# Attention and a gated feed-forward on one core: masks added ahead of the scores, and the casts and loads of the first units reordered

## The chip, the core and the metric

The kernel runs on one core of a Trainium2 chip. A core has five engines with an instruction queue each, which run beside each other and wait for each other through semaphores: TensorE (PE, with its weight loads listed as PEld), VectorE (DVE), ScalarE (ACT), GpSimd (POOL) and SyncE (SP). Transfers between memory and the core go through DMA queues; SyncE, ScalarE and GpSimd issue them. The metric is the device time of one execution in microseconds; lower is better.

## The reference

The inputs are q, k and v (4 batches, 8 heads, 768 positions, 64 values), the list of retrieval heads (0, 2 and 6), and the weights of a feed-forward (512 to 2048 to 512).

```python
scores = scale * np.matmul(q, k.transpose(0, 1, 3, 2))
stream_keep = causal & (is_sink | in_win)        # 4 sink positions, a window of 64
mask = np.where(retr[...], causal, stream_keep)  # by head
a = softmax(np.where(mask, scores, -1e9))
x = (a @ v).transpose(0, 2, 1, 3).reshape(3072, 512)
h = x @ w_in
out = (h * sigmoid(beta * h)) @ w_out
```

## The kernel before, in words

**Units and chunks.** A chunk is one half (384 positions) of one batch; chunks 0 and 1 are the first halves of batches 0 and 1, chunk 2 is the second half of batch 0. Each chunk has four units; unit p handles the two heads p and p+4. So units 0 to 7 are the first two chunks, and there are 32 in all. A retrieval head needs all causal blocks of 128 by 128; a streaming head needs a few, some against a copy of K and V (KO, VO) whose first four rows are the sink.

**What a unit does.** `load_qk` (L123) brings q and k of two units into a staging tile `s`; `load_v` (L143) brings V. `cast` (L286) makes bf16 of them (tile `qkb`). `steps_T` (L361) transposes on TensorE into two PSUM banks (three 128-column transposes for K, three for Q), and copies them out: KT on VectorE (L371), and the two heads' halves of QTP, first on ScalarE, then on VectorE (L378). `sinks_of` (L342) makes KO, on GpSimd for most units. `steps_QK` (L440) cuts the unit's 10 or 11 blocks into three fills; a fill takes one PSUM bank, TensorE computes the scores into it (L464), and ScalarE takes the exponential (L472). `values` (L302) casts V into VX (L300) and makes VO (L313, L314). `steps_PV` (L478) multiplies (L495) and VectorE divides by the sums (L498, L500). `steps_X` (L517) transposes the result into xT.

**Masks.** For units 0 to 7 a masked block gets a second matmul behind its scores, with the identity as weights, which adds a tile of zeros and -1e9 (L469): Nc for a causal diagonal, parts of Ns for streaming heads. Ns and Mc are made by `negatives` (L217). Later units multiply the exponentials by 0 and 1 on VectorE (L437, with Mc and Mh).

**The feed-forward.** `steps_G1` (L550) gives groups of four matmuls x @ w_in (L560), a tanh on ScalarE (L563) and a gate on VectorE (L566). `steps_G2` (L573) gives the second product (L604). `ms(n)` puts n such groups between attention steps. w_in and w_out are cast while they are loaded, by transfers that GpSimd issues (L162, L166).

**Order.** Everything is issued in an order written out by hand for the first units (L706 to L827). Each engine does its instructions in that order, and a queue that waits holds back all that stands behind. PSUM has eight banks; `Banks` hands them out in turn: scores from 0 and 1, idle matmuls, G1 and some fills from 2 to 4, transposes from 5 and 6, PV from 7. A tile in a bank waits until the readers of the tile before it are done. Ten matmuls of zeros (`idle`, L186) stand ahead of everything on TensorE. A load into a staging buffer that was used before waits for a one-column memset by GpSimd (`held=True`).

Of the kernel before, what the change touches and what calls it, by code (L numbers as in the profile page):

```python
# [17 lines left out]
def kernel(  # L18
# [69 lines left out]
    def later(delay, fn):  # L88

        todo = [fn]  # L90

        def once():
            if todo:
                todo.pop()()
        heapq.heappush(heap, (clock[0] + delay, count[0], once))
        count[0] += 1
        return once
# [5 lines left out]
    def step(s):  # L103
        cost, fn = s
        flush(clock[0])
        clock[0] += cost
        fn()
# [15 lines left out]
    def load_qk(c, g, pairs=1, held=False):  # L123

        b, h2 = chunks[c]
        rows = slice(h2 * HALF, (h2 + 1) * HALF)
        both = stage.tile([128, 2, 2, 2, HT, D], F32, name=f"s{g}")
        for i, (name, src) in enumerate((("k", k), ("q", q))):
            staged[name, c, g] = both[:, i]
            if held:  # L130
                nc.gpsimd.memset(staged[name, c, g][:, 0, 0, 0, 0:1], 0.0)
        n = 2 // pairs
        for i in range(pairs):
            for name, src in (("k", k), ("q", q)):
                h = 2 * g + n * i
                eng = nc.scalar if pairs == 2 and name == "q" else nc.sync
                for hs in [slice(0, 2)] if n == 1 else [slice(0, 1), slice(1, 2)]:
                    eng.dma_start(
                        out=staged[name, c, g][:, n * i:n * (i + 1), hs].rearrange("p a h t d -> p (a h) (t d)"),
                        in_=src[b].rearrange("(c a) s d -> a c s d", c=2)[h:h + n, hs, rows, :].rearrange(  # L140
                            "a c (p t) d -> p a c (t d)", t=HT)[:, 0 if n == 1 else slice(0, n), slice(0, 2) if n == 1 else 0])
# [16 lines left out]
    def load_w_in(i, n=1):  # L158
        f = slice(i * 512, (i + n) * 512)
        view = moe_w_in.rearrange("(c a d) f -> c d a f", c=2, a=MO)  # L160
        for c in range(2):
            nc.gpsimd.dma_start(out=w_in_sb[c * D:(c + 1) * D, :, f], in_=view[c][:, :, f])  # L162
# [4 lines left out]
        w_done.add(i)  # L167

    load_qk(0, 0, 2)
    load_qk(0, 1)  # L170
    warm = consts.tile([1, 1], F32, name="warm")
    nc.vector.memset(warm, 0.0)
    nc.scalar.activation(out=warm, in_=warm, func=ACTF.Exp)
# [12 lines left out]
    def idle(n, pool, name):  # L186
        for i in range(n):
            nothing = pool.tile([128, 512], F32, name=name)
            nc.tensor.matmul(nothing, zeros[:, 0:128], zeros, start=True, stop=True)  # L189
    idle(10, ps_m, "mm")  # L190

    def select(buf, cm, step_, base, n):
        nc.gpsimd.affine_select(out=buf, in_=buf, compare_op=ALU.is_ge, fill=0.0, base=base,
# [21 lines left out]
    nc.gpsimd.affine_select(out=Nc, in_=Nc, compare_op=ALU.is_ge, fill=NEG, base=0, pattern=[[1, 128]], channel_multiplier=-1)  # L215

    def negatives():  # L217
        nc.vector.tensor_scalar(out=Mc, in0=Nc, scalar1=0.0, scalar2=None, op0=ALU.is_ge)
        for i, m in enumerate([M0, Mo, Md, Mo, Md]):
            nc.vector.tensor_scalar(out=Ns[:, i * 128:(i + 1) * 128], in0=m, scalar1=-1.0, scalar2=-NEG, op0=ALU.add, op1=ALU.mult)  # L220

# [7 lines left out]

    QTD = [kvp.tile([128, NPAIR, HALF], BF16, name=f"QTD{i}") for i in range(2)]  # L230
    QTP = kvp.tile([128, 3, 2, HALF], BF16, name="QTP")
    QTB = [[QTP[:, i, hh, :] for hh in range(2)] for i in range(3)]

    KT, KO, VX, VO = {}, {}, {}, {}
# [26 lines left out]
    def ones_v(eng, b):  # L261
        for p in range(NPAIR):
            eng.memset(VX[b, p][:, :, :, D:D + 1], 1.0)
            if streams[p]:
                eng.memset(VO[b, p][:, :, :, D:D + 1], 1.0)

    for i in range(3):
        zero_q(i)
    ones_v(nc.vector, 0)
    ones_v(nc.gpsimd, 1)  # L270

    def masks_late(h2):

        m = Mh[h2].rearrange("p (r k j) -> p r k j", r=2, j=128)
        res = []
        if h2 == 0:
            res.append(lambda: nc.vector.tensor_copy(out=m[:, :, 0], in_=M0[:, None, :].to_broadcast([128, 2, 128])))
        n = HT - 1 + h2
        for i, one in ((1 - h2, Mo), (2 - h2, Md)):
            for r in range(2):  # L280
                res.append(lambda i=i, one=one, r=r: nc.vector.tensor_copy(
                    out=m[:, r, i:i + 2 * n - 1:2], in_=one[:, None, :].to_broadcast([128, n, 128])))
        return res
# [12 lines left out]
    def cast_v(u):  # L296
        b, h2, p = units[u]
        c = u // NPAIR
        copy = nc.vector.tensor_copy if u in (0, 1, 2, 3, 5, 7) or 8 <= u < 16 else nc.gpsimd.tensor_copy
        copy(out=VX[b % 2, p][:, h2 * HT:(h2 + 1) * HT, :, 0:D], in_=staged["v", c][:, :, p:H:NPAIR, :])  # L300

    def values(u):  # L302
# [115 lines left out]
    def masks_of(es, lst, h2):  # L418

        res = []  # L420
        i = 0
        while i < len(lst):
            j = i + 1
            if lst[i][5]:
                while j < len(lst) and lst[j][5]:
                    j += 1
                res.append((i, j, Mc[:, None, :].to_broadcast([128, j - i, 128])))
            elif lst[i][6] is not None:
                while j < len(lst) and lst[j][6] == lst[j - 1][6] + 1:
                    j += 1  # L430
                m = lst[i][6]
                res.append((i, j, Mh[h2][:, m * 128:(m + j - i) * 128].rearrange("p (n j) -> p n j", j=128)))
            i = j

        def one(i, j, m):
            e = es[:, i * 128:j * 128].rearrange("p (n j) -> p n j", j=128)
            nc.vector.tensor_mul(e, e, m)  # L437
        return [lambda x=x: one(*x) for x in res]

    def steps_QK(u):  # L440

        b, h2, p = units[u]
        s = st_u.setdefault(u, {})
        s["masks"] = []
        s["blocks"] = blocks = [[[] for _ in range(HT)] for _ in range(2)]
        lst = sum(blocks_of(u), [])
        nb = len(lst)
        nf = -(-nb // 4)
        cuts = [nb * i // nf for i in range(nf + 1)]

        def fill(lo, hi, spare):
            def go():
                s["sinks"]()

                sp = (ps_s3 if u >= 10 else ps_m if spare else ps_s).tile([128, 512], F32, name="sp")
                es = att.tile([128, 512], BF16, name="es", bufs=NES)
                for i in range(lo, hi):
                    blocks[lst[i][0]][lst[i][3]].append((es[:, (i - lo) * 128:(i - lo + 1) * 128], lst[i][4]))
                i = lo
                while i < hi:  # L460
                    j = run_end(lst, i, hi)
                    hh, _, lhs, q0, _, diag, m = lst[i]
                    added = u < 8 and (diag or m is not None)
                    nc.tensor.matmul(sp[:, (i - lo) * 128:(j - lo) * 128], lhs, s["QT"][hh][:, q0 * 128:(q0 + j - i) * 128],  # L464
                                     start=True, stop=not added)
                    if added:

                        neg = Nc if m is None else Ns[:, m % 5 * 128:(m % 5 + 1) * 128]
                        nc.tensor.matmul(sp[:, (i - lo) * 128:(i - lo + 1) * 128], ident, neg, start=False, stop=True)  # L469
                    i = j  # L470
                w = (hi - lo) * 128
                nc.scalar.activation(out=es[:, 0:w], in_=sp[:, 0:w], func=ACTF.Exp, scale=scale)  # L472
                if u >= 8:
                    s["masks"] += [later(700, f) for f in masks_of(es, lst[lo:hi], h2)]
            return ((hi - lo) * (56 if u >= 8 else 95), go)
        return [fill(cuts[i], cuts[i + 1], (u < 4 or u in (6, 7)) and i % 2) for i in range(nf)]

    def steps_PV(u):  # L478
        b, h2, p = units[u]
# [208 lines left out]
    def transposes_of(u):  # L688
        step(steps_T(u)[0])
# [11 lines left out]
    def cast_dp(u):  # L701
        cast(u, "k", dve)
        cast(u, "q")
# [2 lines left out]
    act = nc.scalar.copy  # L706
    cast_dp(0)
    load_v(0, held=True)
    load_qk(1, 0)
    negatives()  # L710
    transposes_of(0)
    st_u[0]["sinks"]()
    cast(1, "k", act)
    cast(1, "q")
    qk = steps_QK(0)
    step(qk[0])
    transposes_of(1)
    step(qk[1])
    step(qk[2])
    st_u[1]["sinks"]()  # L720
    cast_dp(2)
    cast_dp(3)
    qk = steps_QK(1)
    step(qk[0])
    transposes_of(2)
# [8 lines left out]
    step(qk[1])  # L734
    step(qk[2])
    st_u[2]["sinks"]()
    load_qk(1, 1, held=True)
    st_u[3]["sinks"]()
    run(steps_QK(3))
    load_v(1, held=True)  # L740
# [11 lines left out]
    run(steps_PV(3))  # L752
    step(steps_X(1)[0])
    transposes_of(4)
    step(steps_X(2)[0])
    qk = steps_QK(4)
    step(qk[0])
    step(steps_X(3)[0])
    step(qk[1])
    transposes_of(5)  # L760
    nc.vector.memset(w_in_sb[:, 0, 512:513], 0.0)
    step(qk[2])
    qk = steps_QK(5)
    step(qk[0])
    load_w_in(1)
    cast(6)
    cast(7)
    load_w_in(2, 2)
    ms(1)
# [303 lines left out]
```

## Time and profile before

| what | us |
|---|---|
| median of 3 runs | 232.85 (232.28 to 233.64) |
| the profiled execution | 232.27 |
| its span, which the profile shows | 230.6 |
| around the span | 1.67 |
| TensorE busy | 219.8 (95%) |
| ScalarE, VectorE, GpSimd busy | 155.8, 145.1, 100.1 |
| first idle matmul on TensorE | 1.29 |
| first transposes, unit 0 | 5.54 |
| start of the steady run of L560 | 34.98 |

All places in time are microseconds from the start of the span. A line of the timeline has the start, the time until the last of its instructions ends, the engine, the source line, the operation, out<-in, shapes and a count; a bracket gives the idle time of the engine just before it and who ended it. In the windows view a row is a stretch of time: its length, each engine's busy time with its number of instructions, the granted clock, the DMA share and the bytes moved.

### The profile page before, as it was taken

The numbers are of one execution on the slowest core, as the hardware profiler recorded it, in microseconds if no ns is written. First come the engines' busy times: TensorE is split into PE (matmuls) and PEld (weight loads), VectorE is DVE, ScalarE is ACT, GpSimd is POOL, SyncE is SP. The second block draws the span as 40 slices with busy tenths as digits, with TensorE's granted clock in tenths as the row PEclk, the third lists the DMA queues.
The fourth block names the chain that finished last, engine by engine and source line by source line (L and its number), as shares of the span: only waits on it lengthen the run. The fifth ranks groups of instructions, "written<-read, shape, count | busy, mean of one in ns | idle before, by whom it ended". The sixth has DMA issues, their size and how long they took to land.

```text
span 230.6 us, 5311 instructions
## 1 busy us (share of the span) xinstructions
PE 219.8 (95%) x1940; PEld 132.2 (57%) x1960; DVE 145.1 (63%) x367; ACT 155.8 (68%) x304; POOL 100.1 (43%) x218
## 2 busy tenths in 40 slices
PE   7788899999999999999999999999999999999994
PEld 2676675654666666545654565454755556556553
DVE  6795787984768589745954593454781676338700
ACT  2788888882757898567875757684938797128621
POOL 6373780067698999057618692850052000000000
PEclk9999999999999999999999999999999999999999
DMA  6999999999999999968999899962832101211012
GB/s 195 257 183 271 152 155 192 227 209 234 222 185 137 176 135 186 154 133 98 161 194 139 139 182 151 143 126 70 184 53 63 50 0 45 81 47 50 0 45 91
DMA packets 95771, 31.78 MB, mean 138 GB/s; under 512 B 82673, under 2 KB 92289, under 8 KB 95745
## 3 DMA queue, kind: packets, MB, share of 16 engines
q0 software_dynamic: 35424, 8.13, 50.8%
q1 hardware_dynamic: 59456, 22.72, 46.6%
q10 hardware_dynamic: 864, 0.60, 0.8%
q8 instruction: 15, 0.25, 0.5%
q14 instruction: 12, 0.09, 0.2%
HBM read 27.27 MB, written 6.29 MB: 146 GB/s over the span
## 4 chain that ended last, share of the span: by engine, by line
PE 81%; DMA 5%; DVE 5%; ACT 4%; POOL 3%; issue 2%; SPq 1%; ACTq 0%; POOLq 0%
PE tp L604 32%; PE mm L560 31%; PE po L495 5%; PE sp L935 4%; DMA vs<-in_v_dram 3%; PE sp L464 2%; PE mm L189 2%; DMA xT<-x 2%; PE tp L587 2%; PE tp L369 1%; ACT es L939 1%; DVE QTP L378 1%; POOL w_in_sb L162 1%; ACT QTP L378 1%; DVE gT L566 1%
## 5 line engine op out<-in xcount | busy, mean ns | idle before, releaser
L560 PE MATMUL mm<-xT,w_in_sb 128*128 128x384 bf16 x512 | 92.3, 326 | 0.4 <-DMA xT<-x 0.2
L604 PE MATMUL tp<-w_out_sb,gT 128*128 128x512 bf16 x348 | 86.7, 379 | 1.3 <-issue 0.3
L563 ACT ACTIVATE th<-mm,beta_h 128x384 f32<-128x384 f32 x128 | 73.1, 598 | 20.3 <-PE mm L560 14.7
L566 DVE SCALAR_TENSOR_TENSOR gT<-th,mm 128x384 bf16<-128x384 f32 x128 | 67.4, 550 | 30.0 <-ACT th L563 25.7
L560 PEld LDWEIGHTS <-w_in_sb 128*128 128x128 bf16 x512 | 47.9, 98 | 31.7 <-issue 0.6
L604 PEld LDWEIGHTS <-gT 128*128 128x128 bf16 x368 | 33.9, 98 | 33.9 <-issue 0.4
L939 ACT ACTIVATE es<-sp 128x512 bf16<-128x512 f32 (+1 forms) x84 | 39.9, 594 | 4.5 <-PE sp L935 4.5
L611 ACT ACTIVATE osb<-tp 128x512 f32<-128x512 f32 x21 | 12.7, 603 | 31.5 <-PE tp L604 28.4
L472 ACT ACTIVATE es<-sp 128x512 bf16<-128x512 f32 (+1 forms) x44 | 22.9, 560 | 6.1 <-PE sp L464 4.8
L495 PEld LDWEIGHTS <-es 128*128 128x128 bf16 x472 | 20.6, 97 | 8.1 <-issue 0.7
L300 POOL CAST VX<-vs 128x384 bf16<-128x384 f32 x18 | 9.2, 521 | 35.7 <-DMA vs<-in_v_dram 23.4
L326 POOL DMA_DIRECT2D s<-in_q_dram x30 | 22.5, 768 | 0.4 <-issue 0.3
L326 POOL DMA_DIRECT2D s<-in_k_dram x30 | 22.3, 770 | 0.1
L495 PE MATMUL po<-VX,es 128*128 128x65 bf16 x392 | 22.2, 193 | 0.0
L437 DVE TENSOR_TENSOR es<-es,Mh 128x512 bf16<-128x512 bf16 (+3 forms) x58 | 19.4, 368 | 4.4 <-ACT es L939 3.7
L500 DVE TENSOR_TENSOR x<-po,rec 128x384 bf16<-128x384 f32 x32 | 17.8, 558 | 1.1
L464 PE MATMUL sp<-QTP,KT 128*128 128x128 bf16 (+2 forms) x113 | 16.6, 230 | 1.2 <-ACT QTP L378 1.1
L437 DVE TENSOR_TENSOR es<-es,Mc 128x384 bf16<-128x384 bf16 (+2 forms) x21 | 7.3, 351 | 11.3 <-ACT es L939 10.8
L294 POOL CAST qkb<-s 128x384 bf16<-128x384 f32 x14 | 6.8, 510 | 16.7 <-DMA s<-in_q_dram 14.4
L352 POOL COPY KO<-KT 128x128 bf16<-128x128 bf16 (+1 forms) x20 | 8.8, 440 | 9.8 <-DVE KT L371 4.4
L498 DVE RECIPROCAL rec<-po 128x6 f32<-128x6 f32 x32 | 6.1, 191 | 10.2 <-PE po L495 10.1
L464 PEld LDWEIGHTS <-KT 128*128 128x128 bf16 x113 | 10.3, 98 | 3.8 <-DVE KT L371 0.8
(77 smaller groups left out, 174.5 us busy)
## 6 DMA issues: line engine op xcount, KB each, us to landing
vs<-in_v_dram SPq DMA_DIRECT2D x24, 256.0 KB, 6.1
out_dram<-osb SPq DMA_DIRECT2D x23, 256.0 KB, 2.4
s<-in_k_dram SPq DMA_DIRECT2D x12, 192.0 KB, 4.8
w_out_sb<-in_moe_w_out_dram POOLq DMA_DIRECT2D x4, 512.0 KB, 14.5
s<-in_q_dram SPq DMA_DIRECT2D x10, 192.0 KB, 6.1
s<-in_k_dram POOLq DMA_DIRECT2D x30, 64.0 KB, 5.2
s<-in_q_dram POOLq DMA_DIRECT2D x30, 64.0 KB, 5.3
w_in_sb<-in_moe_w_in_dram POOLq DMA_DIRECT2D x4, 256.0 KB, 5.5
```

Source lines behind the costliest of these rows:

```text
L326: nc.gpsimd.dma_start(out=ROWS[c % 2, name][:, t].rearrange("p (a w) -> p a w", a=NPAIR)[:, :, w:w + D], in_=src[b, hh * NPAIR:(hh + 1) * ...
L437: nc.vector.tensor_mul(e, e, m)
L464: nc.tensor.matmul(sp[:, (i - lo) * 128:(j - lo) * 128], lhs, s["QT"][hh][:, q0 * 128:(q0 + j - i) * 128], start=True, stop=not added)
L472: nc.scalar.activation(out=es[:, 0:w], in_=sp[:, 0:w], func=ACTF.Exp, scale=scale)
L495: nc.tensor.matmul(po[:, qi, hh, :], e, val, start=(j == 0), stop=(j == len(lst) - 1))
L500: nc.vector.tensor_mul(x, po[:, :, :, 0:D], rec.to_broadcast([128, HT, 2, D]))
L560: nc.tensor.matmul(hp[:, 0:HALF], w_in_sb[:, mo, fi * 128:(fi + 1) * 128], xT[c][:, mo, :], start=(mo == 0), stop=(mo == MO - 1))
L563: nc.scalar.activation(out=th, in_=hp[:, 0:HALF], func=ACTF.Tanh, scale=beta_h[:, fi:fi + 1])
L566: nc.vector.scalar_tensor_tensor(out=gTs[c][:, fi, :], in0=th, scalar=1.0, in1=hp[:, 0:HALF], op0=ALU.add, op1=ALU.mult)
L604: nc.tensor.matmul(op, gTs[c][:, fi, ns * 128:(ns + 1) * 128], w_out_sb[:, fi, :], start=(fi == 0), stop=(fi == FO - 1))
L611: nc.scalar.activation(out=osb, in_=op, func=ACTF.Copy, scale=0.5)
L939: nc.scalar.activation(out=es[:, 0:w], in_=sp[:, 0:w], func=ACTF.Exp, scale=scale)
```

## The change

It touches how the first eight units start.

- Eight idle matmuls instead of ten.
- Q of chunk 0's second two units is loaded through ScalarE's queue, and the loads of units 2 and 3, 4 and 5, 6 and 7 come in a transfer of their own for each unit and operand, instead of one for two units and one head of the pair.
- In a fill of units 0 to 7 that has masked blocks, the masks are put into the bank first (`pre`), neighbours in one matmul of up to 512 columns, and the scores are added to them. For unit 0 and unit 4 the bank of the first fill is taken earlier.
- Memsets, masks and casts of the first units stand in another order: the QTP memset of unit 2 and the ones of VX and VO later or on GpSimd, Ns before the first cast, Mc much later; unit 1's K cast ahead of unit 0's transposes on ScalarE; unit 1's transposes (in banks 2 and 3) ahead of unit 0's scores; both casts of unit 3 on GpSimd; VX of units 2 and 3 cast by ScalarE instead of VectorE; X(3) transposed in bank 7; unit 7's second fill in the transposes' banks; unit 6's casts ahead of the second load of w_in, whose one-column memset goes.

```diff
-                eng = nc.scalar if pairs == 2 and name == "q" else nc.sync
+                eng = nc.scalar if c == 0 and name == "q" else nc.sync
...
-    load_qk(0, 1)
+    load_qk(0, 1, 2)
...
-    idle(10, ps_m, "mm")
+    idle(8, ps_m, "mm")
...
     def negatives():
-        nc.vector.tensor_scalar(out=Mc, in0=Nc, scalar1=0.0, scalar2=None, op0=ALU.is_ge)
...
+    QKB = {(u, 1): ps_m for u in (0, 1, 2, 3, 6)}
+    QKB[7, 1] = ps_t
...
-    for i in range(3):
+    for i in range(2):
         zero_q(i)
-    ones_v(nc.vector, 0)
-    ones_v(nc.gpsimd, 1)
+    negatives()
...
     def masks_late(h2):
+        if h2:
+            nc.vector.tensor_scalar(out=Mc, in0=Nc, scalar1=0.0, scalar2=None, op0=ALU.is_ge)
...
-        copy = nc.vector.tensor_copy if u in (0, 1, 2, 3, 5, 7) or 8 <= u < 16 else nc.gpsimd.tensor_copy
+        copy = nc.scalar.copy if u in (2, 3) else nc.vector.tensor_copy if u < 2 or u in (5, 7) or 8 <= u < 16 else nc.gpsimd.tensor_copy
...
-        def fill(lo, hi, spare):
+        def fill(i_fill, lo, hi):
+            added = u < 8 and any(x[5] or x[6] is not None for x in lst[lo:hi])
+            got = []
+
+            def pre():
+                if got:
+                    return
+                bank = QKB[u, i_fill] if (u, i_fill) in QKB else ps_s3 if u >= 10 else ps_s
+                got.append(bank.tile([128, 512], F32, name="sp"))
+                i, first_ = lo, True
+                while added and i < hi:
+                    _, _, _, _, _, diag, m = lst[i]
+                    j = i + 1
+                    if diag or m is not None:
+                        while m is not None and j < hi and lst[j][6] == lst[j - 1][6] + 1 and lst[j][6] % 5:
+                            j += 1
+                        neg = Nc if m is None else Ns[:, m % 5 * 128:(m % 5 + j - i) * 128]
+                        nc.tensor.matmul(got[0][:, (i - lo) * 128:(j - lo) * 128], ident, neg, start=first_, stop=False)
+                        first_ = False
+                    i = j
+
             def go():
+                pre()
+                sp = got[0]
                 s["sinks"]()
-                sp = (ps_s3 if u >= 10 else ps_m if spare else ps_s).tile([128, 512], F32, name="sp")
...
-                                     start=True, stop=not added)
-                    if added:
-                        neg = Nc if m is None else Ns[:, m % 5 * 128:(m % 5 + 1) * 128]
-                        nc.tensor.matmul(sp[:, (i - lo) * 128:(i - lo + 1) * 128], ident, neg, start=False, stop=True)
+                                     start=not added, stop=not added or j == hi)
...
     cast_dp(0)
     load_v(0, held=True)
-    load_qk(1, 0)
-    negatives()
-    transposes_of(0)
-    st_u[0]["sinks"]()
+    load_qk(1, 0, 2)
+    ones_v(nc.gpsimd, 0)
     cast(1, "k", act)
     cast(1, "q")
+    transposes_of(0)
     qk = steps_QK(0)
+    st_u[0]["pre"][0]()
+    special[0] = Banks(2, 3)
+    transposes_of(1)
+    special[0] = None
+    zero_q(2)
+    st_u[0]["sinks"]()
     step(qk[0])
-    transposes_of(1)
     step(qk[1])
     step(qk[2])
+    cast_dp(2)
     st_u[1]["sinks"]()
-    cast_dp(2)
-    cast_dp(3)
+    cast(3)
...
-    load_qk(1, 1, held=True)
+    load_qk(1, 1, 2, held=True)
...
     transposes_of(4)
+    qk = steps_QK(4)
+    st_u[4]["pre"][0]()
     step(steps_X(2)[0])
-    qk = steps_QK(4)
     step(qk[0])
+    special[0] = Banks(7)
     step(steps_X(3)[0])
+    special[0] = None
     step(qk[1])
+    ones_v(nc.gpsimd, 1)
     transposes_of(5)
-    nc.vector.memset(w_in_sb[:, 0, 512:513], 0.0)
     step(qk[2])
     qk = steps_QK(5)
     step(qk[0])
+    cast(6)
     load_w_in(1)
-    cast(6)
     cast(7)
     load_w_in(2, 2)
```

More of the change, by code (lines that the diff above doesn't have):

```diff
@@ L462, in go @@
                     hh, _, lhs, q0, _, diag, m = lst[i]
-                    added = u < 8 and (diag or m is not None)
                     nc.tensor.matmul(sp[:, (i - lo) * 128:(j - lo) * 128], lhs, s["QT"][hh][:, q0 * 128:(q0 + j - i) * 128],
-                                     start=True, stop=not added)
-                    if added:
-                        neg = Nc if m is None else Ns[:, m % 5 * 128:(m % 5 + 1) * 128]
-                        nc.tensor.matmul(sp[:, (i - lo) * 128:(i - lo + 1) * 128], ident, neg, start=False, stop=True)
+                                     start=not added, stop=not added or j == hi)
                     i = j
@@ L474, in go @@
                     s["masks"] += [later(700, f) for f in masks_of(es, lst[lo:hi], h2)]
+            s.setdefault("pre", []).append(pre)
             return ((hi - lo) * (56 if u >= 8 else 95), go)
-        return [fill(cuts[i], cuts[i + 1], (u < 4 or u in (6, 7)) and i % 2) for i in range(nf)]
+        return [fill(i, cuts[i], cuts[i + 1]) for i in range(nf)]
     def steps_PV(u):
```

## The prediction, as it was made before the changed kernel ran

> **What bounds the kernel now.** First the windows view, one row for each stretch:
>
> ```profile
> core 0: us, PE busy (x) PEld busy (x) DVE busy (x) ACT busy (x) POOL busy (x), PEclk, DMA share, GB/s
> 5.50:15.50 10.00, 8.14 (x119) 6.79 (x118) 8.14 (x22) 8.39 (x19) 5.22 (x17) 1.00 1.12 231
> 15.50:22.00 6.50, 5.26 (x81) 4.30 (x81) 4.40 (x12) 4.88 (x11) 2.45 (x9) 1.00 1.15 253
> 22.00:28.50 6.50, 5.54 (x62) 3.94 (x60) 4.43 (x10) 5.83 (x12) 5.08 (x11) 1.00 1.07 161
> 28.50:35.00 6.50, 6.24 (x89) 4.54 (x89) 5.61 (x15) 5.04 (x11) 4.75 (x11) 1.00 1.07 154
> 35.00:75.00 40.00, 39.67 (x309) 23.66 (x313) 29.55 (x68) 27.96 (x52) 22.34 (x38) 1.00 1.59 202
> ```
>
> From 35 us on TensorE has almost no gap (39.67 of 40 us). From 5.5 to 35 us it stands idle 1.86 + 1.24 + 0.96 + 0.26 = 4.3 us. So this change, which touches only the first eight units, is worth what it takes off the moment at which the steady matmuls begin (34.98 us), if nothing after that waits for something that does not move with it. Second, TensorE's timeline, whose brackets name the idle time and its releaser:
>
> ```profile
> 1.29 4.45 PE L189 MATMUL mm<-zeros 128*128 128x512 bf16 x10 [1.29 <-DVE zeros L179]
> 5.54 0.85 PE L369 MATMUL tp<-idb,qkb 128*128 128x128 bf16 x6
> ...
> 9.85 0.51 PE L369 MATMUL tp<-idb,qkb 128*128 128x128 bf16 x6 [0.52 <-DVE qkb L294]
> ...
> 19.08 0.33 PE L527 MATMUL tp<-idb,x 128*128 128x128 bf16 x3 [0.27 <-DVE QTP L378]
> ...
> 28.45 0.22 PE L464 MATMUL sp<-QTP,KO 128*128 128x128 bf16 x1 [0.68 <-DVE gT L566]
> ```
>
> The first transposes wait for idle matmuls; unit 2's for a cast; X(3)'s and unit 7's second bank for a PSUM bank that VectorE still reads. The change touches all four.
>
> **The change, step by step.** Times on the left are rows of before, on the right what the same rows give in the new order.
>
> Start. Idle matmuls go out every (5.54 - 1.29)/10 = 0.425 us, so eight end at 4.69. Unit 0's transposes then wait for the K cast (VectorE 4.24 to 4.79) and the Q cast (GpSimd 4.61 + 0.51; the seven memsets ahead of it, 4.33 to 4.61, go, but its load lands at 0.81 + 3.7 = 4.5). They start at 4.84: 0.70 saved of the 0.85. VectorE loses Mc (0.38 until the next instruction) and seven small memsets, but its cast cannot start before the load lands (0.81 + 3.4 = 4.2), so these are worth nothing here.
>
> Unit 1. Its K cast (0.51) moves ahead of ScalarE's QTP copy of unit 0 and waits for a load issued at 1.33, 4.0 us to landing: 5.33 to 5.85. The queued QTP copy runs 5.85 to 6.3 (before 6.42 to 6.9). ScalarE also issues two more loads first (0.5 each), so table load and beta's load slip by 1 us, into ScalarE's idle time (3.05 us before 6.42). Unit 1's transposes end near 6.6, in banks 2 and 3.
>
> VectorE's chain then paces: KT(0) 5.40, QTP(0) 6.30, KT(1) 6.87, QTP(1) 7.45, each 0.57; two QTP memsets of 0.28 moved here, to 8.6; K cast of unit 2 to 9.17. Unit 2's transposes go at 9.22 instead of 9.85: **0.63 saved**. The masks fill TensorE ahead of it, at the same price: a 128-column matmul takes 0.055, a 512-column one 0.217 (L604: four in 0.868), so 30 fewer instructions save under 0.1 us.
>
> Unit 3. Its casts leave VectorE for GpSimd (8.5 to 9.5, done before its transposes at 10.8). From 9.2 on each engine has its old durations: QTP(3) on VectorE ends 12.82 (before 13.54), values begin 12.84, PV(0) on TensorE 13.4 (before 14.15): **0.75**.
>
> Values. ScalarE takes two VX casts between its exponentials, which end at 14.15 (14.85 before), and the two casts of unit 4. No row shows a VX cast on ScalarE; a cast of as many elements took 0.35 on VectorE, 0.51 on ScalarE, 0.53 on GpSimd. I take 0.48, by ScalarE's own cast pitch (0.91 for two). Then VX(3) ends 15.1, GpSimd's VO(3) 15.8 (before 16.0), unit 4's casts 16.0 (before 15.76), the X copies 16.0 and 16.45 (before 16.31, 17.01). So here ScalarE hands back part: QTP(4) at 17.3 instead of 17.96, 0.66. With 0.35 it would be 0.26 earlier, with 0.53 0.1 later.
>
> X(3). In bank 7 it no longer waits until VectorE's QTP(4) has emptied bank 6; TensorE does scores, X(3), masks, scores from 17.8 on and reaches unit 5's transposes at 18.6 instead of 19.69: **1.1**. The first G1 matmul goes at 19.96 instead of 21.22 (1.26: its three masks now precede the wait for QTP(5)).
>
> Unit 6. GpSimd casts it before it issues w_in's second load, not after. Its loads are issued near 13.0 and land 6.0 to 6.2 later, by 19.6; the casts run 20.1 to 21.05 and its transposes need not wait: 22.03 instead of 23.65, **1.6**. The load of w_in that stood first was issued from 21.86, now from 21.05: 0.8 earlier only.
>
> Unit 7. Its second bank is of the transposes' pair and does not wait for the gate at 28.40; it waits for QTP(7), ending 26.02. PV(4) starts at 26.7 instead of 29.22, 2.5. Next is late: the fifth G1 group needs that load of w_in, 22.48 + 6.0 = 28.5 before, 27.7 now. It ran at 29.56: **1.86**. The rest to the steady run (5.4 us) is unchanged, so steady matmuls begin at 33.1 instead of 34.98.
>
> What gives some back. The loads keep up less well. VectorE waits for V of the third chunk, GpSimd behind it issues loads and casts Q of unit 9:
>
> ```profile
> 54.14 0.36 DVE L300 CAST VX<-vs 128x384 bf16<-128x384 f32 x1 [1.28 <-DMA vs<-in_v_dram]
> ...
> 56.75 0.52 POOL L294 CAST qkb<-s 128x384 bf16<-128x384 f32 x1
> ```
>
> Unit 9's transposes ran at 57.88, 0.6 after that cast; TensorE will ask at 56.0, so the cast must come 1.25 earlier. GpSimd's weight loads follow each other without a gap from 21.86 to 51.3 and begin 0.8 earlier; the third chunk's loads are issued some 1.8 earlier. Between 0.8 and 1.8 I take 1.0: a stall of 0.25. Sum: 1.86 - 0.25 = **1.6 us**. The profiled execution took 232.27 (span 230.6 and 1.67 around it), so 230.65 by its side. It is the lowest of the runs shown (median 232.85, to 233.64); the median becomes 231.2.
>
> **Rivals.** *The loads keep their times.* The DMA share is 1.05 to 1.2 in every stretch from 5.5 us on. If the third chunk's V lands at 54.1 as before, unit 9 waits for its cast until 57.3 and only 0.55 us is left: 232.3. Against: the weight queue does start earlier.
>
> *The clock.* The PEclk row says 1.00 from the start, yet 512 columns take 0.425 us at 1.3 and 0.217 later; six transposes took 0.85 at 5.54 and 0.51 at 9.85. TensorE thus starts at half pace and gains the full one between 6.4 and 7.9. If eight idle matmuls and more gaps bring that later, to after 9.2, the 1.5 us of matmuls before unit 2's transposes take 1.5 more, 1.1 of it in the wait for its cast at 8.05 to 9.2; with the work behind at half pace the start's 0.63 is gone: 1.0 left, 231.85. The Trainium skill (TensorE: Matmul & The Clock Gate, Part 1) says that the full clock follows a busy window of about 3.4 us which runs free of the kernel's start; by that, an estimate, two idle matmuls matter only if a window then counts as not busy. No row shows the window.
>
> *Slower.* GpSimd's queue: w_in's second load now stands behind the casts of unit 6, which wait for loads. If these take longer, w_in is late, and with it every G1 group from the fifth on. It is later than before once they land over 9 us after issue (22.4: cast 22.9, second issue 23.5, landing 29.6). The row says 6.0 to 6.2 here, but such loads took 10.4 to 13.4 when issued at 32 to 34.5 beside weight loads. At 11: landing 24.4, cast 24.9, second issue 25.5, w_in at 31.5 instead of its use at 29.56, 1.9 late: 234.8. Against: only w_in's first load (issued 11.4 to 12.8) is beside them.
>
> *The change does nothing*: excluded as a whole, since the order of the instructions moves.
>
> **Chances.** Forecast 0.58, loads 0.19, clock 0.10, slower 0.13. The forecast's own range is 230.4 to 231.7: the VX bounds (+0.3, -0.1), 0.8 to 1.8 for the loads. To leave out no more than 2 in 10 the range reaches over loads and clock, with the spread of the runs shown: 230.0 to 232.9. Half a per cent, 1.16 us, is about what can be told from no change: faster 0.58, within 0.29 (loads, clock), slower 0.13.
>
> **What would show it.** Right: unit 0's transposes at 4.8; unit 2's near 9.2 after VectorE's cast; no wait for QTP(4) before X(3), none for the gate before unit 7's second bank; the steady L560 run from about 33.1; unit 9's transposes at 56 to 56.5. Wrong: half-pace matmuls after 8 us; a wait for w_in_sb at the fifth G1 group beyond 28; ScalarE's casts of unit 4 after 16.3; unit 9's transposes still at 57.

## The result, and the profile after

The changed kernel takes 231.27 us (median of 20 runs, 229.97 to 234.33), the kernel before 232.39 us in runs beside it. The ratio is 0.9947 (95% interval 0.9922 to 0.9971): 0.5% or 1.2 us faster. The forecast was 1.6 us and 231.2 us. Slow executions are left out of the ratios, among them one of the kernel before (288.14 us), two of the changed kernel and the profiled ones of `e3_v_held` (TensorE at half pace from 53.2 to 56.6 us) and `e9_masks_old` (234.13 us), so of these two profiles only early rows are read.

The profiled execution of the changed kernel took 232.34 us, its span 230.6: 15th of its 20 runs from the shortest, and no shorter than the profiled execution before (232.27 and 230.6). So the trace shows both a gain and the place where, in such an execution, it is lost. The windows view of the changed kernel, with the columns as before:

```profile
core 0: us, PE busy (x) PEld busy (x) DVE busy (x) ACT busy (x) POOL busy (x), PEclk, DMA share, GB/s
5.50:15.50 10.00, 8.02 (x120) 6.58 (x121) 7.79 (x22) 8.91 (x21) 5.90 (x20) 1.00 1.20 251
15.50:22.00 6.50, 5.84 (x67) 4.31 (x67) 3.88 (x9) 6.02 (x14) 4.40 (x19) 1.00 1.09 250
22.00:28.50 6.50, 5.88 (x75) 4.34 (x73) 5.29 (x13) 5.46 (x13) 4.90 (x13) 1.00 1.06 151
28.50:35.00 6.50, 6.24 (x68) 4.01 (x65) 5.13 (x12) 5.39 (x11) 2.92 (x6) 1.00 1.08 186
35.00:75.00 40.00, 38.16 (x308) 22.71 (x308) 28.67 (x68) 26.74 (x51) 23.07 (x39) 1.00 1.51 204
```

From 15.5 to 28.5 us TensorE's busy time rises from 10.80 to 11.72. From 35 to 75 us it falls from 39.67 to 38.16: 1.5 us of new idle time in a stretch that the change does not touch. TensorE's timeline names the places:

```profile
4.89 0.53 PE L371 MATMUL tp<-idb,qkb 128*128 128x128 bf16 x6 [0.29 <-DVE qkb L296]
...
8.94 0.51 PE L371 MATMUL tp<-idb,qkb 128*128 128x128 bf16 x6 [0.87 <-DVE qkb L296]
...
17.72 0.33 PE L546 MATMUL tp<-idb,x 128*128 128x128 bf16 x3
18.33 0.50 PE L371 MATMUL tp<-idb,qkb 128*128 128x128 bf16 x6
21.77 0.50 PE L371 MATMUL tp<-idb,qkb 128*128 128x128 bf16 x6
...
26.59 0.43 PE L514 MATMUL po<-VX,es 128*128 128x65 bf16 x9
27.52 0.81 PE L579 MATMUL mm<-xT,w_in_sb 128*128 128x384 bf16 x4 [0.44 <-DMA w_in_sb<-in_moe_w_in_dram]
32.84 15.27 PE L579 MATMUL mm<-xT,w_in_sb 128*128 128x384 bf16 x93 [0.16 <-ACT xT L548]
47.95 0.50 PE L371 MATMUL tp<-idb,qkb 128*128 128x128 bf16 x6
55.74 0.33 PE L371 MATMUL tp<-idb,qkb 128*128 128x128 bf16 x3
57.79 0.34 PE L371 MATMUL tp<-idb,qkb 128*128 128x128 bf16 x3 [1.72 <-POOL qkb L296]
```

X(3) (17.72) has no bracket any more, PV(4) runs at 26.59 instead of 29.22, and the steady run starts at 32.84 instead of 34.98: **2.14 us won at the front**. In the kernel before, TensorE's timeline has units 8 and 9 so, neither with a wait:

```profile
50.09 0.50 PE L369 MATMUL tp<-idb,qkb 128*128 128x128 bf16 x6
...
57.88 0.50 PE L369 MATMUL tp<-idb,qkb 128*128 128x128 bf16 x6
```

Unit 8's transposes are thus still 2.14 us early (47.95 against 50.09). Unit 9's come in two halves; the second waits 1.72 us for a cast of GpSimd. The chain of waits, cut to this stretch, says why the cast is late (start, length, what):

```profile
38.83 15.66 DMA vs<-in_v_dram
54.61 0.37 DVE VX L302
55.03 0.36 POOL VO L315
55.45 0.34 POOL VO L316
55.79 1.43 POOL s L328 x2
57.22 0.52 POOL qkb L296
57.79 0.34 PE tp L371 x3
```

V of the third chunk lands 15.7 us after its issue. Behind VectorE's cast of it stand VO, two load issues and the cast of Q, one after the other on GpSimd. VectorE's timeline shows that it stands still 3.90 us for V, three times as long as before (1.28), that V is cast no earlier than before (54.14), and that it waits for K of the next load as well (1.14; before 1.87):

```profile
54.61 0.36 DVE L302 CAST VX<-vs 128x384 bf16<-128x384 f32 x1 [3.90 <-DMA vs<-in_v_dram]
...
56.57 0.55 DVE L296 CAST qkb<-s 128x384 bf16<-128x384 f32 x1 [1.14 <-DMA s<-in_k_dram]
```

**All of the difference is decided by 63 us.** From unit 10's transposes to the end of the span it is 167.5 us before (63.08 to 230.6), 167.8 after (62.83 to 230.6), and 167.5 to 167.9 in every other profile whose row in the table below is filled. So what is won is what unit 10 starts earlier: 0.25 us in this execution. Worked out from the median (231.27 - 1.67 around the span - 167.7) it is, as an estimate, 61.9 in a middling run, 1.2 earlier than in one of before (232.39 - 1.67 - 167.6 = 63.1).

### The profile page after: what moved, and what is told of

It is laid out like the page before. It is cut to its first block, busy times and chain, and to the rows that moved or that the text cites. A ratio compares the mean times of both kernels' runs of the same rounds, so it can differ in the third digit from the quotient of the medians.

```text
span 230.6 us, 5261 instructions
## 1 busy us (share of the span) xinstructions
PE 219.7 (95%) x1928; PEld 130.3 (57%) x1928; DVE 143.4 (62%) x356; ACT 156.1 (68%) x306; POOL 101.8 (44%) x226
## 4 chain that ended last, share of the span: by engine, by line
PE 71%; DMA 11%; DVE 5%; ACT 4%; SPq 3%; POOL 2%; issue 1%; ACTq 0%; DVEq 0%; POOLq 0%
PE tp L623 31%; PE mm L579 26%; DMA vs<-in_v_dram 7%; PE po L514 5%; PE sp L961 5%; SPq L152 3%; DMA w_in_sb<-in_moe_w_in_dram 3%; DMA s<-in_q_dram 2%; PE sp L486 2%; ACT es L490 2%; PE tp L606 2%; DVE es L439 1%; DVE x L519 1%; DVE gT L585 1%; PE tp L371 1%
## 5 line engine op out<-in xcount | busy, mean ns | idle before, releaser
L623 PE MATMUL tp<-w_out_sb,gT 128*128 128x512 bf16 x368 | 89.3, 379 | 0.0
L439 DVE TENSOR_TENSOR es<-es,Mh 128x512 bf16<-128x512 bf16 (+3 forms) x58 | 20.2, 381 | 4.4 <-ACT es L965 3.7
L486 PE MATMUL sp<-QTP,KT 128*128 128x128 bf16 (+2 forms) x113 | 15.0, 230 | 0.5 <-DVE QTP L380 0.3
L439 DVE TENSOR_TENSOR es<-es,Mc 128x384 bf16<-128x384 bf16 (+2 forms) x21 | 7.8, 370 | 11.4 <-ACT es L965 10.8
L315 POOL COPY VO<-VX 128x128 bf16<-128x128 bf16 (+3 forms) x24 | 9.5, 395 | 10.6 <-DVE VX L302 9.1
L296 POOL CAST qkb<-s 128x384 bf16<-128x384 f32 x15 | 7.5, 520 | 12.5 <-DMA s<-in_q_dram 12.4
```

Of the source, the lines that this page charges most:

```text
L623: nc.tensor.matmul(op, gTs[c][:, fi, ns * 128:(ns + 1) * 128], w_out_sb[:, fi, :], start=(fi == 0), stop=(fi == FO - 1))
```

## The experiments

Each edit is to the changed kernel unless it says otherwise. Ratios are to the kernel before, from runs on the same chip; the other columns come from the one profiled execution of each (us). The start of VectorE's cast of V shows when V landed only where VectorE waited for it (before, changed, e6, e8, e10); in the others V was there earlier.

| kernel | ratio, 95% interval | steady run starts | V of chunk 3 cast | wait at unit 9 | unit 10 | span |
|---|---|---|---|---|---|---|
| before | | 34.98 | 54.14 | 0 | 63.08 | 230.6 |
| changed | 0.9947, 0.9922 to 0.9971 | 32.84 | 54.61 | 1.72 | 62.83 | 230.6 |
| e1_cast9 | 0.9942, 0.9920 to 0.9964 | 34.28 | 52.21 | 0 | 62.48 | 230.0 |
| e2_v_early | 1.0063, 1.0034 to 1.0092 | 34.31 | 53.93 | 0 | 64.47 | 232.2 |
| e3_v_held | 1.0064, 1.0030 to 1.0097 | | | | | |
| e4_half_w_out | 0.9924, 0.9897 to 0.9951 | 33.26 | 51.05 | 0 | 61.35 | 229.0 |
| e5_idle10 | 0.9957, 0.9938 to 0.9976 | 34.83 | 52.62 | 0 | 63.10 | 230.9 |
| e6_x3_bank | 0.9958, 0.9931 to 0.9986 | 33.30 | 53.50 | 0.15 | 61.72 | 229.5 |
| e7_u7_bank | 0.9953, 0.9928 to 0.9977 | 34.09 | 51.88 | 0 | 62.18 | 230.0 |
| e8_w_in_first | 0.9941, 0.9901 to 0.9982 | 32.27 | 50.46 | 0 | 60.36 | 228.0 |
| e9_masks_old | 0.9935, 0.9909 to 0.9960 | | | | | |
| e10_loads_paired | 0.9976, 0.9944 to 1.0007 | 32.54 | 54.61 | 1.97 | 62.84 | 230.7 |
| e11_before_half_w_out | 1.0003, 0.9984 to 1.0022 | 34.97 | 52.77 | 0 | 63.07 | 230.8 |
| e12_cast9_w_in_first | 0.9956, 0.9930 to 0.9982 | 33.03 | 50.95 | 0 | 61.12 | 228.7 |

### What gives the gain back: unit 9

**e1_cast9.** Unit 9's casts right behind unit 8's, ahead of V of the third chunk in the queues.

```diff
     cast_dp(8)
+    cast_dp(9)
...
-        if t == 8:
-            cast_dp(9)
```

> The changed kernel with the two casts of unit 9 moved directly behind those of unit 8, ahead of VX(8), VO(8) and the rows on VectorE and GpSimd. Theory (unit 9 waits only because its Q cast stands on GpSimd behind VO(8), which waits for V of the third chunk): steady matmuls at 32.8 as in the changed kernel, VX(8) still near 54.5, unit 9's transposes at 56.1 instead of 57.8; but KT(9) stands on VectorE behind VX(8) and unit 10's K cast, which waits for a load until 56.6, so unit 9's scores move by about 0.8 us only, and the end by 0.8. Rival (unit 9's own data or a PSUM bank is late): transposes stay at 57.8 and the end does not move.

There is no wait at unit 9 (unit 8 at 49.40, unit 9 at 57.18, 7.78 us as against 7.79 in the kernel before), yet the ratio is that of the changed kernel. This execution does not test the theory, because what it starts from did not occur: V of the third chunk was there by 52.21. V of the *second* chunk was late instead, and PV(4) paid for it. TensorE's timeline:

```profile
28.06 0.43 PE L514 MATMUL po<-VX,es 128*128 128x65 bf16 x9 [1.05 <-POOL VX L302]
```

Up to unit 8's casts this is the changed kernel's own program, so the 2.14 us at the front are no fixed gain: here the steady run starts at 34.28, only 0.70 us earlier than before.

That the order of the casts passes a late V on to unit 9 is seen across the runs. GpSimd's cast of unit 9's Q starts 2.58 to 2.61 us after VectorE's cast of V in the kernel before, the changed kernel, e4, e6, e7, e8, e10 and e11, whether V is cast at 50.46 or at 54.61 (2.92 in e5, 4.82 in e2). In e1 and e12, which part the two, it comes ahead of V.

**e2_v_early** issues V of the third chunk ahead of the loads of w_out instead of behind them.

```diff
+    load_v(2)
     load_w_out(0)
     load_w_out(1)
...
-    load_v(2)
     load_qk(2, 1)
```

> The changed kernel with V of the third chunk issued right behind V of the second (SyncE is free from 20.5 us), ahead of the Q and K loads of the third chunk and of w_out. Theory (V is late because it is issued at 32 to 39 us behind other loads while w_out's loads keep the DMA engines busy): VX(8) no longer waits (50.5 instead of 54.6), unit 9's transposes at 56.1, the whole 1.7 us comes back; price: w_in's second load shares the engines with V, up to 1 us later at the fifth G1 group (27.5). Rival (the DMA engines are full from 20 us on, so what V gains others lose): the fifth G1 group later than 28.5 or unit 8's casts later than 48, and the end not earlier.

Slower than before, 1.0063. TensorE's timeline of it:

```profile
29.00 0.81 PE L579 MATMUL mm<-xT,w_in_sb 128*128 128x384 bf16 x4 [1.78 <-DMA w_in_sb<-in_moe_w_in_dram]
...
51.53 0.34 PE L371 MATMUL tp<-idb,qkb 128*128 128x128 bf16 x3 [1.78 <-POOL qkb L296]
59.16 0.52 PE L371 MATMUL tp<-idb,qkb 128*128 128x128 bf16 x6
```

Unit 9 no longer waits, but the fifth G1 group waits 1.78 us for w_in (0.44 in the changed kernel) and unit 8 another 1.78 for its Q. The same bytes earlier push others later.

**e3_v_held** puts the same load at a place between, behind the last load of w_in and held until its buffer is free.

```diff
     load_w_in(2, 2)
+    load_v(2, held=True)
...
-    load_v(2)
     load_qk(2, 1)
```

> As the one before, but V's issue is held by a memset on GpSimd until w_in's last load is issued (about 24 us). Theory: V lands before 45, unit 9's transposes at 56.1, the fifth G1 group stays at 27.5; 1.7 us back. Rival (DMA engines full): third w_in load late at the seventeenth group (about 38), or unit 8's Q cast, now 43.5, later than 48.

1.0064: slower as well. In the profiled execution unit 8's K transposes (51.24) wait 2.63 us for VectorE's cast and its Q transposes 0.82 for GpSimd's.

**e4_half_w_out** takes bytes away instead of moving them: the last two loads of w_out are left out and that half of w_out is zero, so half of the second product is missing.

```diff
-    load_w_out(2)
-    load_w_out(3)
+    nc.gpsimd.memset(w_out_sb[:, 8:16, :], 0.0)
+    w_done.update((2, 3))
```

> The changed kernel with the third and fourth load of w_out left out; that half of w_out is set to zero by GpSimd instead. Theory of contention (V of the third chunk lands late because it shares the DMA engines with w_out): with 2 of about 4.2 MB less read beside it V lands some 5 us earlier, near 49, unit 9's transposes at 56.1, 1.7 us back. Rival (V's landing is set by its own queue: SyncE's issue or the packets of 256 bytes): VX(8) still near 54.5.

V of the third chunk is there at 51.05, unit 9 does not wait (48.37 to 56.16), and the span is 229.0. The matmuls are all still there, so this fits a unit 9 made late by these bytes; it does not prove it, since e8, below, had V at 50.46 with all of them.

**e11_before_half_w_out** makes the same edit to the kernel before (the same half of the second product is missing).

> The kernel before without the last two loads of w_out; half of w_out is set to zero instead, so the output lacks that half's part. Theory (the bytes of w_out cost the changed kernel something at unit 9 only, because it asks for unit 9 earlier): the kernel before shows no wait at unit 9, so leaving them out is worth nothing to it, 0.999 to 1.001. Rival (fewer bytes help any kernel in the first 57 us, and the 0.5 us between the changed kernel with and without them has nothing to do with the change): 0.997 or less.

1.0003: worth nothing there, as the theory had it. VectorE casts V of the third chunk at 52.77 without a wait (54.14 before, after one of 1.28), yet unit 9's transposes run at 57.87 (57.88 before): in the old order this lateness had a cover, which the 2.14 us won at the front take away. Between the changed kernel and e4 the intervals overlap, so the size of the effect on the median is not settled by these two.

### What the single parts are worth

**e5_idle10**: ten idle matmuls again.

```diff
-    idle(8, ps_m, "mm")
+    idle(10, ps_m, "mm")
```

> The changed kernel with ten idle matmuls again. Theory (TensorE's queue of idle matmuls holds unit 0's transposes, and unit 2's then follow from VectorE's chain): idle matmuls end near 5.4, unit 0's transposes start 0.5 to 0.7 later than 4.9, unit 2's K cast on VectorE and its transposes (8.94) 0.3 to 0.6 later; further on the loads set the pace, so the fifth G1 group (27.52) moves by no more than 0.4 and the time by under 0.3. Rival (the idle matmuls matter through the half-pace start: two more bring the full pace sooner): unit 2's transposes at 8.9 or before.

0.9957: not to be told from the changed kernel. The rival did not show: unit 0's transposes ran at 5.38 instead of 4.89 and unit 2's at 9.43 instead of 8.94, half a microsecond later each; but the later rows of this execution (PV(4) at 28.60, behind a late V of the second chunk) hide it.

**e6_x3_bank**: X(3) in the transposes' banks again.

```diff
-    special[0] = Banks(7)
     step(steps_X(3)[0])
-    special[0] = None
```

> The changed kernel with X(3) in the transposes' banks again. Theory: X(3) (17.72) waits until VectorE's QTP(4) has emptied its bank, 18.1, so unit 5's transposes (18.33) and the first G1 group (19.70) come 0.4 later; the fifth G1 group stays within 0.2 of 27.5, because it waits for w_in, and the time moves by under 0.3. Rival (nothing behind is covered): fifth group and time 0.4 later.

```profile
17.97 0.33 PE L546 MATMUL tp<-idb,x 128*128 128x128 bf16 x3 [0.27 <-DVE QTP L380]
18.58 0.50 PE L371 MATMUL tp<-idb,qkb 128*128 128x128 bf16 x6
```

The wait for QTP(4) is back, in TensorE's timeline above. Unit 2 ran at 8.77 here (8.94 in the changed kernel), unit 5 at 18.58 (18.33): 0.42 us longer between them. That is the bank's part of the 1.36 us by which unit 5 is earlier than before. The time, 0.9958, does not show it.

**e7_u7_bank**: unit 7's second fill in the bank of the G1 groups again.

```diff
-    QKB[7, 1] = ps_t
+    QKB[7, 1] = ps_m
```

> The changed kernel with unit 7's second fill in the banks of G1 again. Theory: it waits for the third gate (25.66 to 26.2) instead of QTP(7) (25.63), so PV(4) starts 0.5 to 0.9 later than 26.59; w_in lands at 27.5 all the same, so the fifth G1 group moves by 0.3 at most. Rival: the whole 0.5 to 0.9 arrives at the fifth G1 group.

```profile
26.23 0.33 PE L470 MATMUL sp<-Ns,idb 128*128 128x256 bf16 x2 [0.51 <-DVE gT L585]
27.86 0.43 PE L514 MATMUL po<-VX,es 128*128 128x65 bf16 x9 [0.69 <-POOL VX L302]
```

The wait for the gate is back with 0.51 us, and behind it PV(4) waits for V of the second chunk in any case: here the transfer, not the bank, sets PV(4). 0.9953.

**e8_w_in_first**: the second load of w_in ahead of unit 6's casts, as before, but without the one-column memset that stood ahead of it.

```diff
+    load_w_in(1)
     cast(6)
-    load_w_in(1)
     cast(7)
```

> The changed kernel with w_in's second load again ahead of unit 6's casts on GpSimd. Theory (in the changed kernel the fifth G1 group waits for that load, 0.4 to 0.8 us): the load is issued near 19.8 instead of 20.7, the casts end at 22.0 instead of 20.7, unit 6's transposes (21.77) 0.3 later, but the fifth group finds w_in at 26.6 and starts no later than 27.5: the reordering of this part is worth nothing or a loss. Rival (the reordering is what wins 0.35 at unit 6): fifth group 0.3 or more later, time later.

Unit 6's transposes ran at 21.70 (21.77 in the changed kernel): the casts did not need the first place. The load was issued at 19.73 instead of 20.70, and the fifth G1 group had no wait for it; the steady run started at 32.27 and the span was 228.0, the shortest of all profiles. The ratio, 0.9941, is still that of the changed kernel.

**e9_masks_old**: each masked block again gets its own mask behind its scores; all else as changed.

```diff
-            added = u < 8 and any(x[5] or x[6] is not None for x in lst[lo:hi])
...
-                        nc.tensor.matmul(got[0][:, (i - lo) * 128:(j - lo) * 128], ident, neg, start=first_, stop=False)
...
+                    added = u < 8 and (diag or m is not None)
...
-                                     start=not added, stop=not added or j == hi)
+                                     start=True, stop=not added)
+                    if added:
+                        neg = Nc if m is None else Ns[:, m % 5 * 128:(m % 5 + 1) * 128]
+                        nc.tensor.matmul(sp[:, (i - lo) * 128:(i - lo + 1) * 128], ident, neg, start=False, stop=True)
```

> The changed kernel with the masks as in the kernel before: each masked block gets its scores first and then its own 128-column mask behind them. Theory (the gain comes from the order of casts, banks and loads, not from the masks): the columns are the same and a 128-column matmul takes 0.055 us, so the first units lose at most 0.3 us, the steady run of G1 matmuls starts within 0.3 us of what the variants so far showed (32.3 to 34.8), and the ratio to the kernel before stays between 0.993 and 0.997. Rival (the masks matter because they fill TensorE's waits for QTP and for casts): unit 1's and unit 3's last fills end 0.3 to 0.7 later, this is carried to the steady run, and the ratio is 0.997 to 0.999.

0.9935: the masks ahead of the scores bring nothing that can be told. Against e12, whose start is equal (unit 0 at 4.90 in both), PV(0) is at 13.02 and 13.04 and unit 5 at 18.13 and 18.16.

**e10_loads_paired**: the loads of units 4 to 7 two units at a time, as before.

```diff
-    load_qk(1, 0, 2)
+    load_qk(1, 0)
...
-    load_qk(1, 1, 2, held=True)
+    load_qk(1, 1, held=True)
```

> The changed kernel with the loads of units 4 to 7 as before, two transfers for two units of one head each instead of one for each unit. Theory (from 20 us on the DMA engines are full, and what counts is when the first of two units is complete): unit 4 and unit 6 become ready only with units 5 and 7; unit 6's casts on GpSimd end up to 1 us later than 22 us, with them the second load of w_in and the fifth G1 group (28.5 to 29.5 instead of 27.5 to 28); ratio 0.996 to 1.000. Rival (the bytes are the same, so the last of them lands at the same time and nothing moves): unit 6's transposes at 21.8 and ratio 0.994 to 0.996.

```profile
21.80 0.50 PE L371 MATMUL tp<-idb,qkb 128*128 128x128 bf16 x6
...
32.54 15.27 PE L579 MATMUL mm<-xT,w_in_sb 128*128 128x384 bf16 x93 [0.16 <-ACT xT L548]
47.65 0.50 PE L371 MATMUL tp<-idb,qkb 128*128 128x128 bf16 x6
55.49 0.34 PE L371 MATMUL tp<-idb,qkb 128*128 128x128 bf16 x3
57.80 0.34 PE L371 MATMUL tp<-idb,qkb 128*128 128x128 bf16 x3 [1.97 <-POOL qkb L296]
```

The theory missed: unit 6 ran at 21.80, no later than with single transfers, and the front was as early as ever. The interval (0.9944 to 1.0007) reaches over both expectations, so the ratio decides nothing. What the timeline shows is the give-back again: the steady run 0.30 us earlier than in the changed kernel, V of the third chunk at 54.61 in both, and unit 9's second half at 57.80 against 57.79. Where V lands late, the front's gain does not reach unit 9.

**e12_cast9_w_in_first**: e1 and e8 together.

> The changed kernel with two edits at once: unit 9's casts right behind unit 8's, and the second load of w_in ahead of unit 6's casts. Theory (two places cap the gain, the fifth G1 group that waits for w_in and unit 9 that waits for its cast, and each can be eased by order alone): no wait for w_in_sb at the fifth G1 group, none at unit 9's transposes, steady run at or before 32.5, time 0.3 to 0.8 us under the changed kernel's, ratio 0.991 to 0.9935. Rival (the loads only trade places, so easing one wait lets another take its place, V of the second chunk or V of the third): ratio 0.994 to 0.996, as every variant so far.

No wait for w_in, none at unit 9, span 228.7; but PV(4) waits 0.22 us for V of the second chunk, and the ratio is 0.9956. The rival held: no version beats the changed kernel by more than the runs can tell, and e4, whose ratio is the lowest, leaves out work.

## Why the prediction was right, and where it missed

**The front was right, within 0.3 us at each step, in this execution.** Unit 0's transposes 4.89 (forecast 4.84), unit 2's 8.94 (9.22), PV(0) 13.22 (13.4), unit 5's 18.33 (18.6), first G1 19.70 (19.96), unit 6's 21.77 (22.03), PV(4) 26.59 (26.7), steady run 32.84 (33.1). ScalarE's VX cast, the unknown, took 0.46 us (0.92 for two) where 0.48 was taken. "Next is late: the fifth G1 group needs that load of w_in" was forecast for 27.7 and came at 27.52 with a bracket that names it.

**The reason for unit 6 was wrong in part.** The 1.6 us there were put down to the casts going ahead of the load of w_in. e8 undoes this order and unit 6 is as early. What e8 and the changed kernel share is that GpSimd is done with the work ahead of both earlier (KO of unit 5 ends at 19.79 in e8, 19.86 in the changed kernel, 21.22 before), and that the one-column memset on VectorE, for which GpSimd waited 0.64 us in the kernel before, is gone. No run parts these two.

**The masks** were priced at under 0.1 us; e9 agrees.

**The give-back was mis-sized.** The stall at unit 9 was taken as 0.25 us, with V of the third chunk some 1.0 earlier. In the profiled execution V landed no earlier and the stall was 1.72, which is the first rival (loads keep their times; unit 9 until 57.3, in fact 57.79) and one of the prediction's own signs of being wrong ("unit 9's transposes still at 57"). In the profiles of e1, e4, e5, e7, e8 and e12 V was there by 52.7 at the latest and there was no stall. So forecast and rival are not two outcomes but two ends of what the runs show.

**A term was missing.** The prediction lets PV(4) start at 26.7 without a wait for V of the second chunk. In e1, e5, e7 and e12 it waits for that load, 0.22 to 1.22 us, and in these four there is no stall at unit 9. GpSimd's timeline of e1, which is the changed kernel's program up to there:

```profile
27.30 0.70 POOL L302 CAST VX<-vs 128x384 bf16<-128x384 f32 x1 [2.29 <-DMA vs<-in_v_dram]
```

The changed kernel and seven of its versions that do all the work (e1, e5, e6, e7, e8, e10, e12) have ratios whose intervals overlap. Their eight profiles, set against the kernel before, have unit 8 earlier by 0.15 to 2.71 us, 1.6 in the mean, and unit 10 by -0.02 to 2.72, 1.0 in the mean. Since each differs by an edit, this is an estimate of a middling run: about 0.3 less at the front than the forecast's 1.86, and about 0.6 given back behind it instead of 0.25. How the changed kernel's own loss parts between front and unit 9 in a middling run stays open, since it has only one trace.

**Some of the closeness is luck.** The forecast of 231.2 us lies 0.07 from the median, but it was worked out from a median of 232.85 for the kernel before, which took 232.39 in the runs beside the changed one. The gain, 1.2 us against 1.6, is the fairer measure, and it hides a loss at two places of which the sum named one.

**The clock rival fell.** The six transposes at 4.89 took 0.53 us, so TensorE was at full pace before unit 0, earlier than in the kernel before (0.85 us at 5.54) with two idle matmuls less. In no profile did the full pace begin after 6.71 (e1); the rival needed 9.2. **The slower rival** needed unit 6's loads to be late; its casts began at 19.80, without a wait.

What stays open: which transfer decides whether V of the third chunk lands at 50.5 (e8) or 54.6 (changed, e10), and whether V of the second is late. Between e8 and these two the order of unit 6's casts and w_in differs, but e1, e5 and e7 have the changed kernel's order and got V by 52.7.

## What to carry to other kernels

A front made faster asks for every later load earlier, while the transfers need not land earlier with it: look for the first load behind the reordered part whose landing is already awaited on an engine off the path (VectorE's 1.28 us here), since its cover shrinks by the whole gain. When the DMA engines are busy throughout (here a DMA share above 1.0 in every stretch from 5.5 to 75 us), moving a load forward may only choose who waits (e2, e3). One profiled execution of such a kernel is one draw: find the place behind which the time is constant (here 167.5 to 167.9 us from unit 10) and compare that.

## What the runs showed that was not expected

**The same load, 3 us apart from run to run.** V of the second chunk was cast by GpSimd at 24.06 without a wait in the changed kernel, at 27.30, after a wait, in e1, whose program is the same up to there, and at 27.85 in e5, which differs by two idle matmuls. GpSimd's timeline of e5:

```profile
27.85 0.70 POOL L302 CAST VX<-vs 128x384 bf16<-128x384 f32 x1 [3.16 <-DMA vs<-in_v_dram]
```

**The full pace of TensorE does not hang on the number of idle matmuls.** In the trace's clock records it began 4.19 us into the span in the changed kernel, 6.41 in the kernel before, and, from e1 to e8, between 4.22 (e2) and 6.71 (e1), both with eight idle matmuls; e5, with ten, had 5.22. The first matmul was at 1.29 each time. The Trainium skill (TensorE: Matmul & The Clock Gate, Part 1) says that the window of about 3.4 us runs free of the kernel's start. The records agree: outside e3 the full-pace stretches last 221.87, 225.28 or 228.69 us, which is 65, 66 or 67 times 3.413 us. The Trainium skill, on the same page, gives half a microsecond to either side for the moment of the change, and here the moments lie 2.5 us apart, less than one such window. In rows: twelve transposes from 4.88 took 1.72 us in e1, twelve from 4.89 1.48 us in e10.
